# A new instruction order for all engines, with GpSimd's first load behind the identity and the integer positions

## The chip, the cores and the metric

The kernel runs on one core of a Trainium2 chip. The metric is the device time of one execution in microseconds, as the median of several runs. The engines are TensorE (PE, with its weight loads as PEld), VectorE (DVE), ScalarE (ACT), GpSimd (POOL) and SyncE (SP); each works through its own list of instructions in order and waits on semaphores for the others.

## The reference

Two stages in a row: attention over a sliding window of 128 keys with a linear bias by distance, and then a token mixer whose weights come from the attention's own output.

```python
# attention: batch 8, heads 8, 576 positions, head size 64
scores = q @ k.T / 8 + slope[h] * -(i - j)        # only where 0 <= i - j < 128
attn   = softmax(scores)
x      = (attn @ v), heads side by side           # batch 8, 576, 512
# mixer
wq, wk = x @ w_q, x @ w_k                         # 512 -> 64
mixed  = ((wq @ wk.T) / 8) @ x
out    = relu(mixed) @ w_out                      # 512 x 512, float32
```

The kernel takes float32 and computes in float16 with float32 sums.

## The kernel before, in words

The work is cut by batch (0 to 7) and, in a batch, by blocks of 128 positions. The names below are those of the operations in the code; `X b.n` means operation X of batch b, block n.

- **Loads.** GpSimd issues nearly all of them: `Lq`, `Lk`, `Lv` for queries, keys and values, `Lt` for the tails (positions 512 to 575) of two batches, `Lw`, `Lwo` for weights. They cast to float16 on the way. Eight of them may be in flight: each waits for the landing of the one eight places ahead. The first blocks of batch 0 (`LF`) come as float32 on the queues of ACT and SP.
- **Transposes.** PE transposes queries and keys (`TF` and `TJ` in batch 0, then `TQ`, `TK`, `TT`); ACT or DVE evicts each result to `qkT` (`EF`, `EJ`, `ETQ`, `ETK`, `ETT`).
- **Softmax.** `QK` makes the scores of one block and half the heads in two banks of PSUM; `EXP` on ACT turns them into exponentials (64 of them, line 657); `MUL` on DVE multiplies by the exponential of the bias, with zero outside the window (32, line 672). That factor, `bias`, is made once: GpSimd writes integer distances (`iota`), DVE turns them into `wm` (`wmc`), ACT takes eight exponentials. `PV` multiplies with the values and with a column of ones (`ones`), which gives the row sums; `RC` and `X` on DVE divide.
- **Mixer**, for two batches at a time: `XT`, `XTT` transpose x; `WQ`, `WK`, `WT` project; `G` is wk.T @ x; `MX` the mixed rows; `RM`, `RMT` the relu; `OUT` the last product; `EO` its eviction; `DO` the store. The last output block is stored as two halves, `OUT7.3a` and `OUT7.3b`.
- `WM` are matmuls on zeros that keep PE busy; `ident` is the identity as float32, `idh` its float16 copy; `zeros` and `pads` are fills.

PSUM is four pairs of banks; `P21` behind a PE operation in the order is pair 2, bank 1, and `P2` the whole pair.

The order of everything is one text, `ORDER`: a list of `name:engine`. `Order.follow` emits the operations in exactly this order, so each engine's list is the subsequence with its letter (P, A, D, G for GpSimd, S for SP). The dependencies of an operation, given as a list in the code, become semaphore waits. Which engine evicts what is part of the text too. The durations given beside the operations in the code do nothing when the kernel is built.

```python
def load(name, want, emits, n, deps):
    return add(*name, want, {"POOL": (0.95 * len(emits), 0.95 * len(emits) + 4.8)}, [ident, *deps],
               lambda o: [e() for e in emits])
```

This helper (line 289) makes every GpSimd load. Its list of dependencies names `ident`, the making of the identity on GpSimd itself.

Of the kernel before, what the change touches and what calls it, by code (L numbers as in the profile page):

```python
# [78 lines left out]
OUT1.1:P31 RC3.0:D RC3.1:D Lk4.2:G X3.1:D EO0.1:A QK4.1.0:P2 X3.0:D TQ5:P1 Lt2:G EXP4.1.0:A
XT3.0:P30 ETQ5:D PV3.2:P0 EO1.1:A PV3.3:P2 EXT3.0:A Lv4.1:G RC3.2:D OUT1.2:P31 X3.2:D Lv4.0:G  # L80
RC3.3:D X3.3:D QK4.0.0:P0 TK5.0:P1 Lk5.2:G EXP4.0.0:A PV3.4:P30 ETK5.0:D XT3.1:P20 Lk5.3:G
RC3.4:D EO1.2:A X3.4:D QK5.0.0:P0 QK5.1.0:P1 MUL4.1:D XTT2:P3 EXP5.0.0:A Lv5.1:G OUT0.0:P21
EXP5.1.0:A EXT3.1:D Lk6.3:G OUT0.3:P00 EXTT2:D EO0.0:A Lk6.2:G MUL4.0:D QK5.0.1:P1 TK4.1:P3
EO0.3:A TT4:P2 Lv5.0:G EXP5.0.1:A OUT1.0:P01 ETK4.1:D Lk6.0:G ETT5:D ETT4:A QK4.2.1:P3 MUL5.0:D
# [12 lines left out]
MUL6.2:D ETT7:A PV5.2:P1 EXP6.0.1:A Lv6.2:G OUT3.2:P30 RC5.2:D ETT6:D X5.2:D Lv7.3:G EO2.2:A
PV5.4:P20 EO3.2:A MUL6.0:D QK6.3.0:P0 TQ7:P1 Lv7.4:G EXP6.3.0:A QK6.1.1:P3 Lv7.0:G OUT3.1:P21
RC5.4:D ETQ7:D EXP6.1.1:A PV5.3:P0 EO3.1:A QK7.0.0:P1 RC5.3:D X5.4:D OUT2.0:P30 Lv6.3:G
EXP7.0.0:A X5.3:D MX2.4:P2 QK7.1.0:P0 EO2.0:A QK6.3.1:P1 RMT2:D EXP7.1.0:A XT5.1:P31 Lv7.2:G  # L100
DO2.0:S MUL6.1:D OUT3.0:P30 DO1.1:S EXP6.3.1:A Lv7.1:G DO1.0:S TK7.1:P0 EXT5.1:D DO1.4:S
QK7.0.1:P2 EO3.0:A PV6.1:P1 ETK7.1:D DO1.2:S EXP7.0.1:A XTT4:P3 DO0.3:S RC6.1:D PV6.2:P0 X6.1:D
DO3.3:S EXTT4:A QK7.3.1:P2 RC6.2:D DO0.0:S MUL7.0:D QK7.3.0:P1 EXP7.3.1:A WK4:P30 DO3.0:S
DO2.2:S EXP7.3.0:A X6.2:D PV6.0:P2 WT4:P31 RC6.0:D MUL6.3:D EWK4:A QK7.2.1:P0 QK7.1.1:P1 EWT4:A
WQ4:P30 X6.0:D EXP7.1.1:A G4:P31 MUL7.3:D EXP7.2.1:A PV6.4:P10 EWQ4:D EG4:A PV7.4:P11
QK7.2.0:P0 RC6.4:D RC7.4:D MX4.4:P3 X7.4:D PV6.3:P2 EXP7.2.0:A X6.4:D OUT3.4:P11 RC6.3:D RMT4:A
X6.3:D MX4.0:P0 MUL7.2:D EO3.4:A MX4.1:P3 XTT6:P2 RM4.0:A XT6.1:P10 DO3.4:S OUT5.4:P11 EXTT6:D
DO3.2:S RM4.1:A MUL7.1:D PV7.3:P0 EO5.4:A MX4.2:P2 RC7.3:D MX4.3:P3 X7.3:D RM4.2:A DO5.4:S
WT6:P11 EXT6.1:D PV7.2:P0 RM4.3:A EWT6:D PV7.1:P2 XT6.0:P10 RC7.2:D X7.2:D OUT4.1:P11 EXT6.0:A
RC7.1:D X7.1:D PV7.0:P0 OUT4.2:P30 RC7.0:D X7.0:D XT7.1:P10 XT7.0:P31 EXT7.1:D OUT5.2:P00  # L110
EXT7.0:A OUT5.3:P10 EO4.1:A WK6:P31 DO4.1:S EO5.3:D DO3.1:S WQ6:P01 EWK6:A EO4.2:A G6:P31
EWQ6:A DO4.2:S DO2.3:S OUT5.0:P01 EG6:A EO5.2:A MX6.0:P3 MX6.4:P1 DO5.2:S MX6.3:P2 RM6.0:D
RMT6:A OUT4.3:P00 EO5.0:A RM6.3:D MX6.1:P1 DO5.0:S EO4.3:A MX6.2:P3 OUT4.0:P01 RM6.2:A DO4.3:S
RM6.1:D DO5.3:S OUT5.1:P00 EO4.0:A OUT7.4:P30 DO4.0:S EO5.1:A OUT7.2:P01 DO5.1:S EO7.4:A
# [960 lines left out]
```

## Time and profile before

| | |
|---|---|
| median of 3 runs | 139.48 us (139.01, 139.48, 140.8) |
| the profiled execution | 138.34 us, of it 136.4 us from its first to its last instruction (the span) |
| TensorE clock granted | 0.993 of full |
| PE busy | 121.7 us (89%) |
| ACT busy | 115.2 us (85%) |
| DVE busy | 107.2 us (79%) |
| GpSimd busy (it issues loads) | 86.3 us (63%) |
| DMA | 24.97 MB, mean 183 GB/s |

The costliest groups are the 64 exponentials on ACT (62.7 us), the 32 multiplications by the bias factor on DVE (38.4 us) and the last product on PE (31.3 us). In the rows of the profile a number in brackets at the end is the time that the engine sat idle before the instruction and what ended it; "issue" means that nothing the profile shows was waited for. In the table of stages each row gives the stretch, its length, the busy time and count of PE, PEld, DVE, ACT and POOL, the granted clock, the share of the DMA engines and GB/s.

### The profile page before, as it was taken

The page shows a single profiled execution, that of the slowest core. Times are in us where ns is not written, and L with a number is a line of the kernel's source. Part 1 is how long each engine was busy: PE and PEld are TensorE (multiplying, and loading weights), DVE is VectorE, ACT ScalarE, POOL GpSimd, SP SyncE. Part 2 cuts the span into 40 slices and gives each one's busy share as a digit, 9 for nine tenths or more (in the row PEclk, how much of TensorE's full clock was granted, in tenths as well). Part 3 has the DMA queues.
Part 4 walks back from the last instruction along what each step waited for, and adds up shares of the span by engine and source line. Part 5 has one row for each costly group of instructions (what it writes and reads, how often), then busy time and mean ns, then how long its engine had stood idle before and what let it go on. Part 6 is the DMA issues. An engine that isn't in the chain of part 4 may idle for free.

```text
span 136.4 us, 5056 instructions
## 1 busy us (share of the span) xinstructions
PE 121.7 (89%) x2173; PEld 78.7 (58%) x2173; DVE 107.2 (79%) x187; ACT 115.2 (85%) x155; POOL 86.3 (63%) x108
## 2 busy tenths in 40 slices
PE   6696797898989799999999999999996999999980
PEld 1453465676757576576486685655765576634440
DVE  4338899999799999999999999997987996245200
ACT  2687998999999999998999998999998684678460
POOL 7999969499969948999999999995100000000000
PEclk9999999999999999999999999999999999999997
DMA  4999999999999999999999999999999570458894
GB/s 99 215 174 169 159 152 183 161 157 142 167 158 170 190 182 153 157 154 157 155 157 153 156 159 143 205 253 177 184 316 361 140 203 0 154 231 304 261 362 154
DMA packets 105414, 24.97 MB, mean 183 GB/s; under 512 B 95536, under 2 KB 100912, under 8 KB 105392
## 3 DMA queue, kind: packets, MB, share of 16 engines
q0 software_dynamic: 96832, 14.42, 149.7%
q1 hardware_dynamic: 6400, 9.05, 19.6%
q10 hardware_dynamic: 2160, 1.18, 2.9%
q8 instruction: 17, 0.28, 0.8%
q14 instruction: 5, 0.04, 0.1%
HBM read 29.62 MB, written 9.44 MB: 286 GB/s over the span
## 4 chain that ended last, share of the span: by engine, by line
PE 49%; DVE 25%; ACT 13%; issue 6%; DMA 3%; SPq 1%; ACTq 0%; DVEq 0%
PE pair L240 40%; DVE pt L672 9%; PE pair L243 9%; ACT pt L657 9%; DVE qkT L254 6%; DVE x L733 5%; DMA osb<-in_q_dram 3%; ACT qkT L252 3%; DVE rm L888 2%; DVE inv L723 1%; ACT osb L252 1%; DVE xT L254 1%; SPq L412 1%; DVE gs L254 1%; DVE xTt L254 0%
## 5 line engine op out<-in xcount | busy, mean ns | idle before, releaser
L657 ACT ACTIVATE pt<-pair 128x1024 f16<-128x1024 f32 x64 | 62.7, 1035 | 3.5 <-PE pair L240 2.6
L393 POOL DMA_DIRECT2D vt<-in_v_dram x40 | 35.7, 962 | 5.5 <-DMA natk<-in_k_dram 2.0
L672 DVE TENSOR_TENSOR pt<-pt,bias 128x2048 f16<-128x2048 f16 x32 | 38.4, 1212 | 0.0
L240 PE MATMUL pair<-wout_sb,rm 128*128 128x512 f16 (+1 forms) x132 | 31.3, 373 | 0.0
L367 POOL DMA_DIRECT2D natk<-in_k_dram x31 | 28.5, 956 | 1.3 <-DMA vt<-in_v_dram 1.1
L240 PE MATMUL pair<-qkT 64*128 64x256 f16 (+2 forms) x320 | 22.6, 250 | 3.7 <-DVE qkT L254 2.6
L240 PE MATMUL pair<-vt,pt 128*128 128x65 f16 (+1 forms) x576 | 22.3, 194 | 3.1 <-issue 0.9
L240 PEld LDWEIGHTS <-pt 128*128 128x128 f16 (+1 forms) x576 | 19.3, 100 | 9.0 <-issue 6.1
L733 DVE TENSOR_TENSOR x<-pair,inv 128x512 f16<-128x512 f32 x32 | 22.0, 689 | 0.9
L252 ACT COPY osb<-pair 128x512 f32<-128x512 f32 (+1 forms) x31 | 17.6, 581 | 4.8 <-PE pair L240 4.2
L240 PEld LDWEIGHTS <-rm 128*128 128x128 f16 x132 | 11.5, 98 | 11.9 <-issue 1.6
L254 DVE COPY qkT<-pair 128x1024 f16<-128x1024 f16 (+2 forms) x25 | 17.3, 700 | 1.3 <-PE pair L243 1.0
L240 PEld LDWEIGHTS <-qkT 64*128 64x128 f16 x320 | 11.4, 94 | 10.7 <-issue 5.0
L379 POOL DMA_DIRECT2D natq<-in_q_dram x12 | 11.5, 1024 | 1.9 <-DMA natq<-in_q_dram 1.6
L886 ACT ACTIVATE rm<-pair 128x1024 f16<-128x1024 f32 x11 | 10.8, 1025 | 0.1
L243 PE MATMUL pair<-identh,x 128*128 128x128 f16 x128 | 9.7, 219 | 0.4 <-DVE x L733 0.4
L252 ACT COPY qkT<-pair 128x1024 f16<-128x1024 f16 (+2 forms) x8 | 8.5, 1088 | 0.9 <-PE pair L243 0.6
L888 DVE TENSOR_SCALAR rm<-pair 128x1024 f16<-128x1024 f32 x5 | 5.9, 1220 | 3.9 <-PE pair L240 3.9
L243 PEld LDWEIGHTS <-x 128*128 128x128 f16 x128 | 7.7, 97 | 2.2 <-issue 1.0
L252 ACT COPY xT<-pair 128x1024 f16<-128x1024 f16 x6 | 6.2, 1027 | 2.9 <-PE pair L243 2.9
L723 DVE RECIPROCAL inv<-pair 128x8 f32<-128x8 f32 x32 | 6.3, 200 | 2.3 <-PE pair L240 1.7
L240 PE MATMUL pair<-warm 128*128 128x512 f16 x21 | 6.6, 439 | 1.3 <-DVE warm L295 1.2
(69 smaller groups left out, 136.9 us busy)
## 6 DMA issues: line engine op xcount, KB each, us to landing
out_dram<-osb SPq DMA_DIRECT2D x29, 256.0 KB, 4.0
vt<-in_v_dram POOLq DMA_DIRECT2D x32, 128.0 KB, 7.1
natk<-in_k_dram POOLq DMA_DIRECT2D x31, 128.0 KB, 6.5
natq<-in_q_dram POOLq DMA_DIRECT2D x4, 512.0 KB, 7.6
natq<-in_q_dram POOLq DMA_DIRECT2D x12, 128.0 KB, 5.7
out_dram<-osb SPq DMA_DIRECT2D x8, 128.0 KB, 2.5
vt<-in_v_dram POOLq DMA_DIRECT2D x8, 64.0 KB, 5.3
natt<-in_q_dram POOLq DMA_DIRECT2D x4, 128.0 KB, 5.7
```

The source lines that it names most:

```text
L240: hold(nc.tensor.matmul(*a, **k))
L243: hold(nc.tensor.transpose(*a))
L252: hold(nc.scalar.copy(out_ap, in_ap))
L254: hold(nc.vector.tensor_copy(out=out_ap, in_=in_ap))
L367: return lambda: nc.gpsimd.dma_start(out=natk(b, n), in_=k[b, :, P * n:P * n + P, :].transpose([1, 0, 2]))
L379: return lambda: nc.gpsimd.dma_start(out=rows_q(b)[:, r], in_=q[b, :, 0:512, :].rearrange("h (p r) d -> r p h d", r=QR)[r])
L393: return lambda: nc.gpsimd.dma_start(out=vtv(b, t)[:n, :, 0:D], in_=v[b, :, P * t:P * t + n, :].transpose([1, 0, 2]))
L657: nc.scalar.activation(out=pt, in_=two(hold_.bank).rearrange("p e c -> p (e c)"), func=AF.Exp, scale=SCALE)
L672: nc.vector.tensor_tensor(out=pv, in0=pv, in1=bt, op=ALU.mult)
L733: nc.vector.tensor_tensor(out=x_s[b % NX][qt].rearrange("p (g h d) -> p g h d", g=2, h=4), in0=sums(p)[:, :, :, 0:64], in1=box["inv"].unsq ...
L886: hold(nc.scalar.activation(out=out_ap, in_=in_ap, func=AF.Relu, scale=WSCALE))
L888: hold(nc.vector.tensor_scalar(out=out_ap, in0=in_ap, scalar1=0.0, scalar2=WSCALE, op0=ALU.max, op1=ALU.mult))
```

## The change

Three edits. Each load names `iota` as a dependency beside `ident`. The numbers of `WM` matmuls per place are others (22 in all instead of 21). And `ORDER` is a new text: the same 693 operations in another order, with 44 of them on another engine or queue. Of the evictions of the last product (`EO`), 24 instead of 31 are on ACT and 13 instead of 6 on DVE. The order was found by a search in whose model an instruction fetch takes long until the loads have ended; nothing of that search is in the kernel.

```diff
-WARM = (5, 10, 1, 2, 1, 2,)
+WARM = (6, 9, 1, 1, 2, 3,)
...
     def load(name, want, emits, n, deps):
-        return add(*name, want, {...}, [ident, *deps],
+        return add(*name, want, {...}, [ident, iota, *deps],
```

The start of the order:

```diff
-warm:D LF0.0.0.0:A LF0.0.1.0:S ones.2:D ident:G LF0.0.0.1:A LF0.1.0.1:S LF0.0.1.1:A ones.3:D
-LF0.1.0.0:S Lv2.4:G iota:G Lq0.2:G wmc:D Lk0.2:G WM.0:P31 TF0.0.0:P00 ones.0:D Lk0.1:G
-TF0.1.1:P01 EF0.0.0:A Lq1.0:G bias:A TF0.1.0:P00 Lk1.0:G EF0.1.0:D idh:D Lk1.1:G ones.1:D
-Lv0.1:G WM.1:P31 TJ0.2.0:P00 EF0.1.1:A Lv0.0:G TF0.0.1:P10 EJ0.2.0:A QK0.0.0:P2 Lk1.2:G
-EF0.0.1:D EXP0.0.0:A pads:D TJ0.1.1:P3 QK0.0.1:P1 Lk1.3:G TJ0.2.1:P0 zeros:D EXP0.0.1:A
+warm:D LF0.0.0.0:A LF0.0.1.0:S ones.2:D iota:G LF0.0.1.1:A LF0.1.0.0:S ident:G LF0.0.0.1:A
+zeros:D LF0.1.0.1:S Lv2.4:G ones.1:D Lq0.2:G pads:D Lk0.2:G wmc:D WM.0:P31 TF0.0.0:P00 Lk0.1:G
+ones.3:D bias:A Lq1.0:G ones.0:D TF0.0.1:P01 idh:D Lk1.0:G TF0.1.1:P10 EF0.0.1:D Lk1.1:G
+TF0.1.0:P11 EF0.1.1:D Lv0.0:G EF0.0.0:A EF0.1.0:A Lk1.2:G Lk1.3:G WM.1:P31 TJ0.2.1:P1
+QK0.0.1:P0 QK0.0.0:P2 EJ0.2.1:D Lv0.1:G TJ0.2.0:P30 EXP0.0.0:A TJ0.1.1:P1 EJ0.2.0:D Lk0.3:G
+EXP0.0.1:A QK0.2.1:P3 EJ0.1.1:D QK0.2.0:P2 QK0.1.1:P1 EXP0.2.1:A MUL0.0:D TQ1:P0 EXP0.2.0:A
```

PE alone, from the projection WK4 of batches 4 and 5 to the first products of batch 7:

```diff
-WK4 PV6.0 WT4 QK7.2.1 QK7.1.1 WQ4 G4 PV6.4 PV7.4 QK7.2.0 MX4.4 PV6.3 OUT3.4 MX4.0 MX4.1
-XTT6 XT6.1 OUT5.4 PV7.3 MX4.2 MX4.3 WT6 PV7.2 PV7.1 XT6.0 OUT4.1 PV7.0
+WK4 PV6.1 PV6.2 QK7.3.0 WQ4 PV6.4 QK7.3.1 QK7.2.1 QK7.2.0 G4 PV6.3 OUT3.4 PV7.4 MX4.4 MX4.1
+MX4.0 XT6.0 OUT5.4 MX4.2 XTT6 MX4.3 XT6.1 WT6 PV7.2 PV7.3 OUT4.2 PV7.0
```

The loads from the last of batch 6's keys on, with the stores that open the store queue:

```diff
-... Lq7.03 Lk7.3 DO2.1 Lk7.2 DO1.3 DO0.1 Lv6.0 DO0.2 Lv6.1 Lv6.2 Lv7.3 Lv7.4 Lv7.0 Lv6.3 Lv7.2 DO2.0 DO1.1 Lv7.1 DO1.0 ...
+... Lv7.3 Lk7.2 Lk7.3 Lv6.2 Lv6.0 DO3.3 Lv6.1 DO0.2 DO2.1 Lv6.3 DO0.1 DO1.3 Lv6.4 DO1.0 Lv7.0 DO0.0 Lv7.4 Lv7.2 Lv7.1 DO3.0 ...
```

The end of the order:

```diff
-EO7.0:A OUT7.3a:P30 EO7.3b:A DO7.0:S DO7.3b:A EO7.3a:A DO7.3a:A
+DO6.1:S EO6.3:D OUT7.1:P30 DO6.3:S EO7.0:A OUT7.3b:P10 DO7.0:S EO7.1:A OUT7.3a:P11 EO7.3b:D
+DO7.1:S DO7.3b:A EO7.3a:A DO7.3a:S
```

More of the change, by code (lines that the diff above doesn't have):

```diff
@@ L79 @@
[L79 to L84, printed above, removed]
@@ L97 @@
[L97 to L102, printed above, removed]
@@ L103 @@
[L103 to L114, printed above, removed]
@@ new lines @@
+TK4.1:P3 OUT0.3:P21 EXP5.0.0:A Lk6.0:G ETK4.1:D TT4:P1 EO0.0:D EO0.3:A Lq6.02:G XTT2:P3
+QK5.1.1:P0 ETT5:D ETT4:A OUT1.0:P20 EXTT2:D Lk6.2:G EXP5.1.1:A MUL4.1:D PV4.0:P3 Lk6.1:G
+QK4.2.0:P1 EO1.0:A QK4.2.1:P0 RC4.0:D WK2:P21 EXP4.2.0:A X4.0:D Lv5.1:G MUL5.1:D OUT1.4:P20
+EXP4.2.1:A Lk6.3:G PV4.1:P1 MUL5.0:D EWK2:A Lq6.01:G EO1.4:A TK5.1:P0 QK4.3.0:P3 Lv4.3:G
+WQ2:P21 RC4.1:D EXP4.3.0:A X4.1:D Lq6.00:G ETK5.1:D WT2:P20 EWQ2:A QK4.3.1:P3 MUL4.2:D EWT2:A
+Lq6.03:G QK5.2.0:P0 PV5.0:P1 EXP4.3.1:A G2:P20 Lk7.0:G RC5.0:D X5.0:D EXP5.2.0:A Lv4.4:G
@@ new lines @@
+MUL4.3:D QK5.2.1:P3 XT4.0:P21 EG2:A Lk7.1:G PV4.2:P0 EXP5.2.1:A EXT4.0:D MX2.3:P1 Lq7.02:G
+RC4.2:D MX2.2:P2 RM2.3:A X4.2:D TK6.1:P3 Lt3:G ETK6.1:D TK6.0:P0 RM2.2:A PV5.1:P1 ETK6.0:D
+MX2.0:P3 RC5.1:D PV4.3:P0 Lq7.01:G X5.1:D RM2.0:A QK5.3.1:P2 RC4.3:D TQ6:P1 Lv5.2:G X4.3:D
+EXP5.3.1:A MX2.1:P3 ETQ6:D QK5.3.0:P0 Lq7.03:G RM2.1:A XT4.1:P20 Lq7.00:G PV4.4:P21 EXT4.1:D
+EXP5.3.0:A TK7.0:P1 QK6.1.0:P3 Lv5.4:G ETK7.0:D OUT3.3:P20 EXP6.1.0:A RC4.4:D Lv5.3:G X4.4:D
+QK6.1.1:P1 MUL5.2:D QK6.2.1:P0 QK6.2.0:P3 Lv7.3:G EXP6.1.1:A OUT2.1:P21 Lk7.2:G EXP6.2.0:A
@@ new lines @@
+XT5.0:P10 OUT2.3:P11 Lk7.3:G EO2.1:A EXT5.0:D EXP6.2.1:A MUL5.3:D PV5.2:P3 Lv6.2:G OUT2.2:P10
+EO3.3:A Lv6.0:G RC5.2:D EO2.3:A DO3.3:S X5.2:D TT6:P2 EO2.2:A TQ7:P0 Lv6.1:G DO0.2:S ETT6:D
+QK6.0.1:P3 ETT7:D DO2.1:S QK6.0.0:P1 ETQ7:D Lv6.3:G EXP6.0.1:A PV5.4:P20 DO0.1:S OUT3.2:P21
+DO1.3:S Lv6.4:G EXP6.0.0:A RC5.4:D DO1.0:S MUL6.1:D QK6.3.0:P0 Lv7.0:G DO0.0:S PV5.3:P3
+EXP6.3.0:A OUT3.1:P10 X5.4:D Lv7.4:G RC5.3:D EO3.2:A X5.3:D Lv7.2:G QK6.3.1:P0 EO3.1:A
+QK7.1.0:P2 MUL6.0:D MX2.4:P3 EXP6.3.1:A XT5.1:P11 Lv7.1:G OUT2.0:P10 RMT2:D EXP7.1.0:A EXT5.1:D
@@ new lines @@
+TK7.1:P0 QK7.0.0:P3 EO2.0:A XTT4:P2 MUL6.2:D OUT3.0:P11 EXTT4:A EXP7.0.0:A ETK7.1:D WT4:P10
+QK7.1.1:P2 MUL6.3:D EWT4:A QK7.0.1:P3 PV6.0:P0 EXP7.1.1:A WK4:P10 RC6.0:D X6.0:D EXP7.0.1:A
+PV6.1:P2 MUL7.1:D PV6.2:P0 EO3.0:A QK7.3.0:P3 EWK4:A RC6.2:D DO3.0:S RC6.1:D WQ4:P11 X6.2:D
+EXP7.3.0:A DO1.1:S X6.1:D PV6.4:P10 DO1.2:S EWQ4:A QK7.3.1:P0 DO2.3:S RC6.4:D QK7.2.1:P2 X6.4:D
+QK7.2.0:P3 EXP7.3.1:A DO0.3:S MUL7.0:D G4:P11 DO1.4:S EXP7.2.1:A DO2.2:S MUL7.3:D PV6.3:P0
+DO2.0:S EG4:A OUT3.4:P10 DO3.1:S EXP7.2.0:A RC6.3:D X6.3:D PV7.4:P11 EO3.4:A MX4.4:P2 MX4.1:P3
@@ new lines @@
+RC7.4:D MX4.0:P0 X7.4:D RMT4:A XT6.0:P10 RM4.1:D RM4.0:A OUT5.4:P11 EXT6.0:D MX4.2:P0 EO5.4:A
+XTT6:P3 MX4.3:P2 MUL7.2:D EXTT6:A XT6.1:P10 RM4.3:A WT6:P11 RM4.2:D PV7.2:P3 EXT6.1:A PV7.3:P2
+EWT6:D OUT4.2:P00 RC7.2:D X7.2:D PV7.0:P1 OUT5.3:P01 RC7.3:D RC7.0:D X7.3:D PV7.1:P3 X7.0:D
+XT7.1:P20 RC7.1:D OUT4.3:P10 X7.1:D EO5.3:D XT7.0:P11 EO4.3:A OUT4.1:P21 DO5.3:S EXT7.0:D
+EXT7.1:A DO5.4:S EO4.2:D OUT5.1:P10 DO3.2:S WK6:P20 EO5.1:D DO5.1:S WQ6:P10 EWK6:A DO3.4:S
+G6:P20 EWQ6:D OUT5.0:P10 EG6:A EO4.1:A MX6.4:P0 MX6.0:P3 EO5.0:D DO4.1:S MX6.3:P2 RM6.0:A
@@ L289, in load @@
     def load(name, want, emits, n, deps):
-        return add(*name, want, {"POOL": (0.95 * len(emits), 0.95 * len(emits) + 4.8)}, [ident, *deps],
+        return add(*name, want, {"POOL": (0.95 * len(emits), 0.95 * len(emits) + 4.8)}, [ident, iota, *deps],
                    lambda o: [e() for e in emits])
```

68 lines of the change are left out of this document (30 added, 38 removed).

## The prediction

> **What bounds the kernel now.** I read the page first (busy time, queues), then a table of stages, then the start instruction by instruction, then the loads and the one long unexplained pause of PE.
>
> ```profile
> span 136.4 us, 5056 instructions
> ...
> PE 121.7 (89%) x2173; PEld 78.7 (58%) x2173; DVE 107.2 (79%) x187; ACT 115.2 (85%) x155; POOL 86.3 (63%) x108
> ...
> q8 instruction: 17, 0.28, 0.8%
> ```
>
> The stages below are cut where the work changes: start, first softmax stage, second, last, tail. Each pair after the length is an engine's busy time and its instruction count.
>
> ```profile
> 0.00:16.00 16.00, 11.68 (x147) 6.60 (x148) 8.85 (x25) 10.87 (x17) 14.93 (x24) 1.00 1.61 163
> 16.00:62.00 46.00, 41.40 (x886) 29.15 (x885) 43.86 (x71) 44.11 (x53) 39.02 (x48) 1.00 2.16 164
> 62.00:89.50 27.50, 26.95 (x526) 17.71 (x516) 26.75 (x45) 26.42 (x36) 27.50 (x33) 1.00 2.34 163
> 89.50:110.40 20.90, 19.73 (x421) 13.37 (x421) 18.51 (x33) 18.96 (x28) 4.81 (x6) 1.00 1.50 240
> 110.40:132.40 22.00, 21.96 (x204) 11.88 (x203) 9.23 (x16) 14.50 (x24) 0.00 (x0) 1.00 0.59 210
> ```
>
> The order is PE, weight load, DVE, ACT, POOL. No engine bounds everything. From 16 to 62 us DVE (43.86 of 46) and ACT (44.11) are both nearly full; from 62 to 89.5 us PE, DVE, ACT and POOL all are; in the tail PE alone is (21.96 of 22.00). What a new order can win is the idle time of the start, some two microseconds of DVE and ACT idle between 89.5 and 110.4 us, and nothing in the tail.
>
> The loads run close ahead of their users. One key block of batch 5 and the transposes (TK5.0) that use it:
>
> ```profile
> L367 POOL DMA_DIRECT2D natk<-in_k_dram x1: 896/896/896, 55.0 to 55.0; - x1
> ...
> DMA to landing us min/median/max: 6.3/6.3/6.3
> ...
> 61.73 0.40 PE L243 MATMUL pair<-identh,natk 64*128 64x64 f16 x16
> ```
>
> Issued at 55.0, landed at 61.3, used at 61.73: 0.4 us of slack. PE does not wait, but work that came earlier here would.
>
> **The start.** The change puts the two iotas ahead of the identity and the first load behind both, and reorders DVE, ACT and PE.
>
> ```profile
> 1.25 0.28 DVE L321 MEMSET vt<- 64x264 uint32 x1
> 1.44 0.81 POOL L393 DMA_DIRECT2D vt<-in_v_dram  x1
> ...
> 1.74 0.09 DVE L322 MEMSET vt<- 128x40 f16 x1 [0.21 <-DVE vt L321]
> ...
> 2.26 0.39 POOL L309 IOTA wint<- 128x256 int32 x1
> ...
> 2.58 0.27 POOL L310 IOTA wint<- 128x128 int32 x1
> 2.76 0.75 POOL L371 DMA_DIRECT2D natq<-in_q_dram  x1
> 2.88 0.36 DVE L316 TENSOR_SCALAR wm<-wint 128x384 f32<-128x384 int32 x1 [0.37 <-POOL wint L310]
> ...
> 3.86 0.56 DVE L318 SCALAR_TENSOR_TENSOR wm<-wm,wint 128x384 f32<-128x384 f32 x1
> ...
> 5.41 3.41 ACT L336 ACTIVATE bias<-wm 128x384 f16<-128x384 f32 x8
> ...
> 10.51 0.69 DVE L254 CAST qkT<-pair 128x512 f16<-128x512 f32 x1 [1.85 <-PE pair L243]
> ...
> 10.84 1.94 ACT L657 ACTIVATE pt<-pair 128x1024 f16<-128x1024 f32 x2
> ...
> 11.87 0.55 DVE L326 MEMSET qkT<- 128x256 uint32 x2
> ...
> 12.75 0.94 PE L240 MATMUL pair<-qkT 64*128 64x256 f16 x12 [0.99 <-DVE qkT L254]
> ...
> 13.51 1.02 ACT L657 ACTIVATE pt<-pair 128x1024 f16<-128x1024 f32 x1 [0.73 <-PE pair L240]
> ```
>
> GpSimd: both iotas together fill 2.26 to 2.85, so the first load moves from 1.44 to about 2.03. It was followed by the iotas before, and is followed by the query tail's load at once now: 2.03 + 0.81 = 2.84 against 2.76. Every later load therefore moves by 0.1 us at most. The one that is really late by 0.6 us is the last value block of batch 2, which nothing uses before batch 2's last product. Cost: 0 to 0.1.
>
> DVE: the positions are ready some 1.4 us earlier, but `wmc` now stands behind two `ones` (0.58 each, 1.25 to 1.83), `zeros` (0.55) and `pads` (four small memsets; 0.6 is an estimate from the one at 1.74 and the gap before it): 1.25 + 0.58 + 0.55 + 0.58 + 0.6 = 3.6, and its three steps (2.88 to 4.42, 1.54) end at 5.2 instead of 4.42. ACT no longer evicts a transpose ahead of the bias, so the eight exponentials run 5.2 to 8.6 instead of 5.41 to 8.82. Behind them come the two evictions (0.6 and 0.35, estimates from the casts in this stage) and one QK (0.39 per four matmuls): the first EXP starts near 10.05 instead of 10.84.
>
> The third EXP now waits for 32 small transposes (0.7) and one cast (0.69) behind that QK: 10.0 + 0.7 + 0.7 + 0.4 gives 11.9, which is before the second EXP ends at 12.0. The 0.73 us of ACT idle at 13.51 goes, and so does the 0.99 us that PE waited at 12.75, since `pads` and `zeros` no longer stand between it and the DVE copies. I carry the first EXP's 0.8 us as the head start; the bounds are 0 (the bias chain is late by what I estimated for `pads`) and 1.5 (the third EXP).
>
> **Where the head start goes.** Up to the last product of batch 3 the new order moves evictions between ACT and DVE: four of keys or queries or x (0.68, 0.70, 1.23, 0.69), two of 0.42 come to DVE, five (0.68, 0.69, three of 0.42) leave it, by the means of these shapes: 4.14 - 2.63 = +1.5 us for DVE, about -3 for ACT. DVE then has 43.86 + 1.5 = 45.4 us of work. At the share it reaches in the next stage (26.75 of 27.5, 97.3%) that needs 46.6 us, 0.6 more than the 46 of now. Head start -0.8, plus 0.6: -0.2 at 62 us. The loads say the same from the other side: the first 50 keep their places to within a few, batch 5's first keys stand at the same place, and their slack is 0.4, less 0.1 for the later start. I take **-0.25**, with ends of -0.4 (slack used up) and +0.8 (DVE only as full as now, 43.86 of 46, 95.3%: 47.6 us needed, +1.6, less 0.8). From 62 to 89.5 us the lists hold the same work on all engines to within 1 us: 0.
>
> **The pause of PE.** Between 89.5 and 110.4 us PE stops once for long, and names nothing that it waits for:
>
> ```profile
> 96.31 0.66 PE L240 MATMUL pair<-vt,pt 128*128 128x65 f16 x16
> ...
> 97.73 0.73 PE L240 MATMUL pair<-qkT 64*128 64x192 f16 x16
> ...
> 98.39 1.11 PE L240 MATMUL pair<-wqk_sb,xT 128*128 128x64 f16 x32
> ...
> 100.73 1.05 PE L240 MATMUL pair<-xT,wqk_sb 128*64 128x512 f16 x8
> ...
> 101.61 1.03 PE L240 MATMUL pair<-x,wk 128*64 128x512 f16 x8
> ...
> 102.48 0.39 PE L240 MATMUL pair<-xtl,wkt 128*64 128x256 f16 x4
> 102.70 0.42 PE L240 MATMUL pair<-vt,pt 128*64 128x65 f16 x16
> ...
> 103.69 0.39 PE L240 MATMUL pair<-qkT 64*128 64x256 f16 x4
> ...
> 105.33 0.57 PE L240 MATMUL pair<-vt,pt 128*128 128x65 f16 x13 [0.92 <-issue]
> ...
> 105.73 1.02 PE L240 MATMUL pair<-wout_sb,rmt 128*128 128x512 f16 x4
> ```
>
> It stops inside one product (three of its 16 matmuls before, 13 after), so no operand is missing. I read it as a late block of instructions: the instruction queue moved 17 blocks of 16 KB (0.28 MB), and PE has 2 x 2173 = 4346 instructions, 256 to a block, that is 128 matmuls with their weights. The block that ended here began some 12 matmuls into WK4 (98.39). It was used up at 104.41 = 105.33 - 0.92, 6.02 us after WK4's start; the next one was there after 6.94.
>
> In the new order the block starts in WK4 too, but holds other work: WK4 1.11, PV6.1, PV6.2 and PV6.3 0.66 each, two QK of group 3 0.73, WQ4 1.05, G4 1.03 + 0.39, PV6.4 0.42, two QK 0.39 each, OUT3.4 1.02, and ends at PV7.4. That sums to 8.5 us. The operations that fill it now (WK4, PV6.0, WT4, two QK, WQ4, G4, PV6.4, PV7.4, a QK, MX4.4) sum to 7.15 by their rows and took 6.02, since neighbours overlap; at the same ratio 8.5 becomes 7.15. That is more than 6.94: the fetch fits by 0.2 us, and the pause goes. DVE and ACT both idle around it, so it lies on the path. Gain **-0.9**; ends -0.9 and 0.
>
> The Trainium skill's page "Runtime: NRT & Kernel Launch" (Instruction fetch mechanics) says that the next block is fetched while the current one runs, 256 instructions at a time, and that crossing into it is mostly hidden; the block size agrees with this trace, "hidden" does not agree with the 0.92. By that rule the pause has another cause, the gain is 0, and the sum is -0.25.
>
> **The tail** after 110.4 us holds the same PE work in both orders from PV7.2 on, but that PV7.3 stands there in place of XT6.0 (0.66 against some 0.6); PE has no idle to give. Seven evictions move from ACT to DVE, which has 12.8 us free there (22.00 - 9.23): 0. Of the last two half stores ACT still issues one ahead of its last eviction: 0 to -0.1.
>
> **Sum.** -0.25 - 0.9 = -1.15: span 136.4 to 135.25. The profiled execution's own time is 138.34, of which 1.94 lies around the span, so 137.2. The median of the runs shown is 139.48, 1.14 above the profiled one; the same step from there gives **138.3 us**.
>
> **Rivals.**
>
> *More stores ahead of the last loads (slower).* The store queue opens with four stores now, behind which it waits; with seven in the new order.
>
> ```profile
> natq<-in_q_dram POOLq DMA_DIRECT2D x12, 128.0 KB, 5.7
> ...
> 85.33 2.55 SPq L993 DMA_DIRECT2D out_dram<-osb  x4
> ...
> L393 POOL DMA_DIRECT2D vt<-in_v_dram x1: 1191/1191/1191, 86.3 to 86.3; - x1
> ...
> DMA to landing us min/median/max: 8.4/8.4/8.4
> ```
>
> The value load issued at 86.3 behind four stores took 8.4 us instead of 5.7: 0.7 a store, 2.0 for three more. It landed at 94.7, the next some 0.9 later, and the product at 96.31 needs both: 0.7 of slack. So +1.3 once batch 6's value loads land later than their product's turn, and the fetch stays late behind the same traffic: -0.25 + 1.3 is +1.05, **140.5**. Against it: the store queue now opens behind a later eviction, by then about three more loads are through. 0.2.
>
> *DVE takes over* in 16 to 62 us: +0.8 - 0.9 = -0.1, **139.4**. For it: DVE would have 0.6 us idle in 46. 0.12.
>
> *The pause is no late fetch, or moves to another block's end*: only -0.25, **139.2**. For it: the margin of 0.2 us; and the page named above. 0.16.
>
> *The order runs as planned in the last two stages as well*: -0.4 at 62, and ACT's idle of 1.08 + 1.94 = 3.0 between 62 and 110.4 falls to 1.0, pause included, -2.0: **137.1**. For it: ACT and DVE still wait some 1 us there beside the pause. 0.17.
>
> **How the numbers follow.** The forecast has 0.35. The two nearest rivals lie between it and no change, so 137.1 to 140.5 are the cases; with 0.6 beyond either end for the spread of the runs (139.01 to 140.8 before) the range is 136.4 to 141.0. A measurement of this kernel tells about 2% from no change, here 2.8 us: under 136.7 is reached only if the fast rival goes somewhat further, 0.12; over 142.3 only if the stores cost twice what I gave them, 0.07; within 0.81.
>
> **What would show it.** Right: the first EXP near 10.0 us, no ACT idle of 0.7 before the third; DVE over 97% busy from 16 to 62 us; TK5.0 at 61.3 to 61.6; PE without a pause named "issue" over 0.3 us after 95 us; the tail from PV7.2 as long as now (22 us). Wrong: PE waiting for value loads near 97 us with landings over 9 us; a pause of 0.5 us or more at another place between 85 and 110; or a DVE stretch over 98% from which ACT idles longer than now.

## The result, and the profile after

The new kernel takes 137.91 us (median of 20 runs, 136.91 to 139.82) against 138.97 us for the kernel before in the same session (20 runs, 137.66 to 141.44): a ratio of 0.9929, interval 0.99 to 0.9958. That is 1.06 us less, inside the two per cent that count as no change. Ratios, here and below, compare only the executions in the faster of the two states in which each kernel runs, so they differ a little from the ratios of the medians. The forecast was 1.2 us less. The profiled execution took 137.62 us, 135.4 us of it the span.

The page of the new kernel, the lines that answer to those shown of before, and the share of the engines in the chain that ended last, below it the same line of before:

```profile
span 135.4 us, 5054 instructions
...
PE 122.8 (91%) x2174; PEld 78.1 (58%) x2174; DVE 114.0 (84%) x197; ACT 107.3 (79%) x145; POOL 86.3 (64%) x108
...
q8 instruction: 17, 0.28, 0.8%
...
PE 67%; DVE 13%; ACT 10%; DMA 3%; issue 3%; ACTq 1%; DVEq 0%
```

```profile
PE 49%; DVE 25%; ACT 13%; issue 6%; DMA 3%; SPq 1%; ACTq 0%; DVEq 0%
```

Some 7 us of work moved from ACT to DVE (ACT has 7.9 us less, DVE 6.8 more). In the chain PE has 67% (49% before), DVE 13% (25%) and "issue" 3% (6%). The same five stretches in the table of stages:

```profile
0.00:16.00 16.00, 12.30 (x142) 7.09 (x144) 8.65 (x26) 9.41 (x16) 14.73 (x24) 1.00 1.60 162
16.00:62.00 46.00, 41.60 (x904) 29.07 (x898) 44.81 (x72) 42.75 (x53) 39.48 (x48) 1.00 2.17 165
62.00:89.50 27.50, 27.06 (x549) 17.39 (x549) 25.53 (x43) 26.44 (x37) 27.50 (x33) 1.00 2.41 154
89.50:110.40 20.90, 20.87 (x414) 13.70 (x414) 20.57 (x33) 20.49 (x30) 4.63 (x6) 1.00 1.36 253
110.40:132.40 22.00, 20.92 (x180) 10.80 (x178) 14.40 (x26) 8.18 (x13) 0.00 (x0) 1.00 0.64 222
```

In 16 to 62 us DVE is at 44.81 of 46, which is 97.4%. In 89.5 to 110.4 PE is at 20.87 of 20.90 (19.73 before): there the pause is gone.

The start did not go as forecast. TensorE's timeline, and then ACT's, in the new kernel (start, duration, the group, and the idle time with what ended it):

```profile
3.80 1.10 PE L243 MATMUL pair<-ident,osb 128*128 128x128 f32 x4
6.56 2.02 PE L243 MATMUL pair<-ident,osb 128*128 128x128 f32 x8 [1.65 <-DMA osb<-in_q_dram]
8.40 2.92 PE L240 MATMUL pair<-warm 128*128 128x512 f16 x9
11.25 0.29 PE L243 MATMUL pair<-identh,natk 64*128 64x64 f16 x8
```

```profile
5.12 3.41 ACT L336 ACTIVATE bias<-wm 128x384 f16<-128x384 f32 x8 [1.40 <-DVE wm L318]
8.44 0.83 ACT L252 CAST qkT<-pair 128x512 f16<-128x512 f32 x2
12.02 6.59 ACT L657 ACTIVATE pt<-pair 128x1024 f16<-128x1024 f32 x7 [2.75 <-PE pair L240]
```

The bias chain was early (5.12, forecast 5.2), but TF0.0.1 waited 1.65 us for a first block that landed at 6.51, and behind it nine zero matmuls stood ahead of the first QK. The first EXP came at 12.02, not 10.05, which is 1.18 us later than in before's profile (10.84). From it on, ACT runs without the 0.73 us gap ahead of the third EXP.

The block of instructions that starts in WK4, on TensorE's timeline, and the waits of PE from 60 us on, of the new kernel:

```profile
97.88 1.09 PE L240 MATMUL pair<-wqk_sb,xT 128*128 128x64 f16 x32
...
104.01 1.02 PE L240 MATMUL pair<-wout_sb,rmt 128*128 128x512 f16 x4
104.97 0.44 PE L240 MATMUL pair<-vt,pt 128*64 128x65 f16 x16
```

```profile
PE pair L240 <- ACT pt L657: 0.3, 1, 0.3
```

No "issue" is among them (0.9 before). Between the two profiled executions the difference comes late: TK5.0 starts at 61.60 (61.73 before), PV5.4 at 89.51 (89.53), PV7.2 at 109.15 (110.41), the last product OUT7.3a at 130.72 (131.77). The experiments show that this pair of executions isn't the whole story.

### The profile page after: what moved, and what is told of

Its sections match the earlier page's. It is cut to its first block, busy times and chain, and to the rows that moved or that the text cites. A ratio compares the mean times of both kernels' runs of the same rounds, so it can differ in the third digit from the quotient of the medians.

```text
span 135.4 us, 5054 instructions
## 1 busy us (share of the span) xinstructions
PE 122.8 (91%) x2174; PEld 78.1 (58%) x2174; DVE 114.0 (84%) x197; ACT 107.3 (79%) x145; POOL 86.3 (64%) x108
## 4 chain that ended last, share of the span: by engine, by line
PE 67%; DVE 13%; ACT 10%; DMA 3%; issue 3%; ACTq 1%; DVEq 0%
PE pair L240 54%; PE pair L243 12%; ACT pt L657 6%; DVE pt L672 4%; DVE qkT L254 4%; DMA osb<-in_q_dram 3%; DVE x L733 3%; ACT qkT L252 2%; DVE rm L888 1%; ACTq L412 1%; ACT rm L886 1%; DVE inv L723 1%; ACT wqT L252 0%; DVE xT L254 0%; ACT gs L252 0%
## 5 line engine op out<-in xcount | busy, mean ns | idle before, releaser
L254 DVE COPY qkT<-pair 128x1024 f16<-128x1024 f16 (+2 forms) x27 | 19.3, 734 | 4.1 <-PE pair L243 3.9
L252 ACT COPY osb<-pair 128x512 f32<-128x512 f32 (+1 forms) x24 | 14.0, 596 | 10.5 <-PE pair L240 9.7
L254 DVE COPY osb<-pair 128x512 f32<-128x512 f32 (+1 forms) x13 | 8.7, 668 | 5.1 <-PE pair L240 5.1
L240 PE MATMUL pair<-warm 128*128 128x512 f16 x22 | 7.8, 491 | 1.5 <-DVE warm L295 1.2
L254 DVE COPY xT<-pair 128x1024 f16<-128x1024 f16 x11 | 7.5, 685 | 1.2 <-PE pair L243 1.1
L243 PE MATMUL pair<-identh,natk 64*128 64x64 f16 x248 | 6.5, 191 | 1.2 <-ACT pt L657 0.9
L243 PEld LDWEIGHTS <-natk 64*128 64x128 f16 x248 | 5.3, 94 | 3.9 <-issue 3.3
```

The costliest lines, as they stand in the source:

```text
L240: hold(nc.tensor.matmul(*a, **k))
L243: hold(nc.tensor.transpose(*a))
L252: hold(nc.scalar.copy(out_ap, in_ap))
L254: hold(nc.vector.tensor_copy(out=out_ap, in_=in_ap))
```

## The experiments

Ratios are to the kernel before on the same chip, whose medians there were 139.02 us (e1 to e4), 139.02 us (e5, e6, h1, h2) and 138.77 us (e7, e8, h3, h4); the new kernel itself was not run beside them. Each kernel ran 12 times, e3, h2 and h4 six times. Where only places in the order change, the diff gives the moved words. Line numbers in the experiments are one lower than in the two kernels.

### The pause alone

**e1.** OUT3.4 is moved forward in the order of before, to lengthen the block:

```diff
-... G4 ... MX4.4 ... PV6.3 ... OUT3.4 ... EO3.4 ...
+... G4 OUT3.4 ... EG4 EO3.4 ... MX4.4 ... PV6.3 ...
```

> The order of before with one product moved: OUT3.4 (four matmuls, 1.02 us) and its eviction stand right behind G4 instead of behind PV6.3, so they lie inside the block of 256 PE instructions that starts in WK4 and ended in a pause of 0.92 us. Late fetch (my theory): the block takes about 0.9 us longer, the pause shrinks from 0.92 to under 0.2 us, and the kernel gains 0.6 to 0.9 us, ratio to before 0.993 to 0.996. Rival, the pause has another cause or PE was only waiting for others there: the pause stays or the idle time turns up elsewhere, ratio 0.998 to 1.002.

Measured: 139.68 us, ratio 1.0029 (0.9996 to 1.0063). The pause is gone from the profile, but two waits for ACT of 0.30 and 0.41 us stand in the same stage. The runs show no gain from the edit. That it took the pause away is not shown either: e5 and e6 below leave this stretch of before's order as it is, and their profiles have no pause. (The profiled execution of e1 ran at half the granted clock from 16.1 to 19.6 us, so I read its waits and not its sums.)

**e2.** Nine stores of before are moved behind DO3.4 on the store queue, so that the last loads have the DMA engines to themselves:

```diff
-... DO0.2 DO2.0 DO1.1 DO1.0 DO1.4 DO1.2 DO0.3 DO3.3 DO0.0 DO3.0 DO2.2 DO3.4 ...
+... DO0.2 DO1.1 DO3.4 DO2.0 DO1.0 DO1.4 DO1.2 DO0.3 DO3.3 DO0.0 DO3.0 DO2.2 ...
```

> The order of before with nine of the ten stores that run between 94 and 103 us moved behind DO3.4 on the store queue (about 107 us). Nothing else differs. Late fetch behind DMA traffic: with the stores gone from the queues the instruction block comes earlier than 6.9 us after the start of WK4, the pause is under 0.3 us, the last value loads land 2 to 4 us earlier than 109 us, and the gain is 0.5 to 0.9 us (ratio 0.993 to 0.996). Rival, the fetch takes as long without the stores (it is late by its own, and only a longer block cures it): the pause stays at 0.7 us or more and the ratio is 0.998 or above.

Measured: 139.53 us, ratio 1.0037 (1.0007 to 1.0068). The last load landed at 101.1 us instead of 109.1, and the pause moved one block ahead, into WK4 itself (TensorE's timeline of e2):

```profile
99.95 0.49 PE L239 MATMUL pair<-wqk_sb,xT 128*128 128x64 f16 x11
100.94 0.77 PE L239 MATMUL pair<-wqk_sb,xT 128*128 128x64 f16 x21 [0.50 <-issue]
```

Less traffic from stores doesn't cure it. One matmul group of equal operations is cut in two here, exactly 128 matmuls before the place of the pause in before: that fits the end of a block of instructions, as the prediction read it.

**e4.** The same step the other way: OUT3.4 is moved back in the new order.

```diff
-... PV6.3 ... OUT3.4 ... PV7.4 EO3.4 MX4.4 ...
+... PV6.3 ... PV7.4 MX4.4 OUT3.4 EO3.4 ...
```

> The changed kernel with OUT3.4 and its eviction moved out of the block of instructions again, from before PV7.4 to behind MX4.4. The block that starts in WK4 then takes about 6.1 us instead of 7.1. If the new order cured the pause by the length of the block: a pause named issue of 0.5 to 0.9 us comes back near PV7.4, and the ratio to before rises from 0.993 to 0.997 to 1.000. If it was cured because the stores stand elsewhere and the fetch itself comes earlier (it landed 4.3 us after the start of WK4 in the changed kernel, 5.5 in the one before): no pause over 0.2 us, ratio 0.991 to 0.995.

Measured: 138.89 us, ratio 0.9971 (0.9935 to 1.0006). TensorE's timeline of e4:

```profile
104.07 0.66 PE L239 MATMUL pair<-vt,pt 128*128 128x65 f16 x16
105.24 0.44 PE L239 MATMUL pair<-vt,pt 128*64 128x65 f16 x16 [0.51 <-DVE pt L671]
```

No pause comes back although the block is shorter again. Instead PV7.4 waits 0.51 us for MUL7.3. In the new order OUT3.4 covers that wait. From WK4 to PV7.2 this profile takes 12.31 us against 11.27 in the new kernel's, so the place of OUT3.4 is likely worth something, but not because it lengthens a block. The runs alone do not show it: the interval of e4 overlaps that of the new kernel.

### The start

**e3.** The new kernel with eight of the nine zero matmuls of the second place moved to the first.

```diff
-WARM = (6, 9, 1, 1, 2, 3,)
+WARM = (14, 1, 1, 1, 2, 3,)
```

> The changed kernel with eight of the nine matmuls on zeros that stand before the first key transposes (8.4 to 11.3 us) moved to the very start (14 there, 1 here; 22 in all, so the instruction blocks keep their places). The first EXP should start about 9.7 to 10.2 us instead of 12.0. Loads set the pace (my theory): by TK5.0 (61.60 us) the head start is down to 0.5 us or less, and the time is that of the changed kernel within 0.4 us, ratio to before 0.989 to 0.994. Rival, the head start is kept: 1.5 to 2 us less, ratio 0.978 to 0.983. A third way: PE runs colder in the first transposes and is slower, ratio above 0.995.

Measured: 136.91 us, ratio 0.9856 (0.9814 to 0.9899). That interval lies just below the new kernel's own (0.99 to 0.9958): with six runs, in another session than the new kernel's, this version beats before and very likely the new kernel too. TensorE's timeline of e3, then ACT's:

```profile
1.19 5.70 PE L239 MATMUL pair<-warm 128*128 128x512 f16 x14 [1.19 <-DVE warm L294]
6.73 2.44 PE L242 MATMUL pair<-ident,osb 128*128 128x128 f32 x12
8.99 0.40 PE L239 MATMUL pair<-warm 128*128 128x512 f16 x1
...
12.95 1.08 PE L242 MATMUL pair<-identh,natq 128*64 128x128 f16 x32 [0.34 <-DMA natq<-in_q_dram]
...
18.11 0.62 PE L242 MATMUL pair<-identh,natk 64*128 64x64 f16 x16 [1.11 <-DMA natk<-in_k_dram]
```

```profile
10.40 3.77 ACT L656 ACTIVATE pt<-pair 128x1024 f16<-128x1024 f32 x4 [0.82 <-PE pair L239]
```

The zeros fill the wait for the first blocks, the first EXP comes at 10.40, and then PE waits for loads (0.34 and 1.11 us), which the new kernel with its late start doesn't. TK5.0 comes at 61.86, no earlier than in the new kernel. But this profile shows e3 at its worst: the granted clock fell to half from 20.0 to 23.4 us, and of the six runs the profiled one is the slowest (138.13 us, the others 136.42 to 137.01). How far the others kept their lead no profile shows.

**e8.** The new kernel with eight of the same zeros left out.

```diff
-WARM = (6, 9, 1, 1, 2, 3,)
+WARM = (6, 1, 1, 1, 2, 3,)
```

> After with one zero matmul instead of nine at the second place (6, 1 instead of 6, 9; the variant with 14, 1 had the ratio 0.9856). Theory 1, the zeros only delay: the first EXP comes at 10.0 to 10.6 us, ratio 0.984 to 0.988, as good as with the zeros moved ahead. Theory 2, the zeros are needed to bring TensorE to its full rate early: the first EXP comes at 11 us or later, matmuls of the head take twice as long until some 13 us, ratio 0.993 to 1.000.

Measured: 138.18 us, ratio 0.9978 (0.9934 to 1.0021). TensorE's timeline of e8:

```profile
8.24 0.61 PE L239 MATMUL pair<-warm 128*128 128x512 f16 x1
9.32 0.40 PE L242 MATMUL pair<-identh,natk 64*128 64x64 f16 x8 [0.47 <-ACT qkT L251]
...
13.08 1.08 PE L242 MATMUL pair<-identh,natq 128*64 128x128 f16 x32 [0.42 <-DMA natq<-in_q_dram]
...
32.90 0.29 PE L242 MATMUL pair<-identh,natk 64*128 64x64 f16 x8 [0.33 <-DMA natk<-in_k_dram]
```

In its profile the start is as early as e3's (first EXP at 10.45) and loads are waited for as late as 32.90; its runs, on another chip, are not as good as e3's. Leaving the zeros out is not the same as running them earlier.

**e7.** The same for before.

```diff
-WARM = (5, 10, 1, 2, 1, 2,)
+WARM = (5, 1, 1, 2, 1, 2,)
```

> Before with one zero matmul instead of ten at the second place (WM.1), so that nothing stands in front of TJ0.2.0. Theory 1, these zeros delay work that is ready: TJ0.2.0 starts at about 8.0 us (its identity is made by 7.97) instead of 8.97 to 12.0, the first EXP comes near 10 to 10.8 us whichever rate TensorE has, and the ratio is 0.988 to 0.995. Theory 2, the zeros are what brings TensorE to its full rate; without them the transposes and QK of the head run at half rate to 13 us or more, and the ratio is 1.000 to 1.005.

Measured: 138.97 us, ratio 1.0048 (1.0009 to 1.0088). TensorE's timeline of e7:

```profile
8.06 1.06 PE L242 MATMUL pair<-identh,natq 64*64 64x64 f16 x32 [0.30 <-DVE identh L312]
...
10.12 0.61 PE L239 MATMUL pair<-qkT 64*128 64x256 f16 x4
...
13.86 1.92 PE L242 MATMUL pair<-identh,natq 128*64 128x128 f16 x32
```

The work starts earlier and runs at half speed: the same 32 transposes take 1.92 us here and 1.08 in e8's row, four QK 0.61 instead of 0.39. Here too the zeros cannot simply be left out; the first theory falls.

**e6.** Before with nine zeros moved to the first place.

```diff
-WARM = (5, 10, 1, 2, 1, 2,)
+WARM = (14, 1, 1, 2, 1, 2,)
```

> Before, with nine of the ten zero matmuls of the second place moved to the first (14, 1 instead of 5, 10). Theory 1, a start that is late passes through to the end, and what makes it late is the second group of zero matmuls in front of work that is ready (2.3 us in the profile of before, more where PE runs at the slow start-up rate): the first EXP comes no later than 10.8 us and the ratio is 0.993, the same step as between the new kernel with and without this edit (0.9856 against 0.9929). Theory 2, the step there came only from the new order's first transposes, which wait for a late landing in front of the zeros: ratio 1.000 here. Theory 3, in before the zeros are run in idle time of PE and the first group, grown by nine, delays TF0.0.0: 1.003 to 1.007.

Measured: 138.36 us, ratio 0.9974 (0.9938 to 1.001). ACT's timeline of e6:

```profile
7.63 0.59 ACT L251 CAST qkT<-pair 128x512 f16<-128x512 f32 x1 [3.92 <-PE pair L242]
8.11 3.42 ACT L335 ACTIVATE bias<-wm 128x384 f16<-128x384 f32 x8
```

In this order ACT evicts TF0.0.0 ahead of the bias, so the longer first group of zeros delays the bias from 5.41 to 8.11, and the first EXP comes at 12.59. In the new order the bias stands first and isn't touched. That would explain why the same edit gains 0.7% there and nothing certain here.

**e5.** Before with the iotas ahead of the identity, the part of the change in its title.

```diff
-... ident:G LF0.0.0.1:A ... LF0.1.0.0:S Lv2.4:G iota:G Lq0.2:G ...
+... iota:G ident:G LF0.0.0.1:A ... LF0.1.0.0:S Lv2.4:G Lq0.2:G ...
```

> Before, with only the two iotas put ahead of the identity on GpSimd; the first load then stands behind both, as in the new kernel. Theory 1, the head's lead is lost in front of the loads' pace: the eight bias exponentials start up to 0.7 us earlier (4.7 instead of 5.41), the first EXP at 10.1 to 10.8, TK5.0 at 61.5 to 61.8 as before, ratio 1.000. Theory 2, an early start passes to the end: ratio 0.995. Theory 3, the identity comes 0.6 us later and with it the first transposes and all loads: ratio 1.003 to 1.005.

Measured: 138.46 us, ratio 0.9975 (0.994 to 1.0009). By itself it gives nothing that can be told from no change: in this order the bias still stands behind EF0.0.0 and started at 5.45 (5.41 before). Its profile is of more use for what it shows of an execution of before's order. TensorE's timeline of e5, then ACT's; below them the one row of before's timeline that answers to it:

```profile
5.87 0.67 PE L242 MATMUL pair<-ident,osb 128*128 128x128 f32 x2 [0.50 <-DMA osb<-in_q_dram]
6.36 4.44 PE L239 MATMUL pair<-warm 128*128 128x512 f16 x10
10.72 0.69 PE L242 MATMUL pair<-identh,natq 64*64 64x64 f16 x32
...
99.97 1.11 PE L239 MATMUL pair<-wqk_sb,xT 128*128 128x64 f16 x32
...
106.22 1.02 PE L239 MATMUL pair<-wout_sb,rmt 128*128 128x512 f16 x4
```

```profile
12.59 1.94 ACT L656 ACTIVATE pt<-pair 128x1024 f16<-128x1024 f32 x2
15.27 3.77 ACT L656 ACTIVATE pt<-pair 128x1024 f16<-128x1024 f32 x4 [0.74 <-PE pair L239]
```

```profile
6.70 2.34 PE L240 MATMUL pair<-warm 128*128 128x512 f16 x10
```

The ten zeros take 4.44 us here and 2.34 in before's profile. PE's rate, and not the place of the iotas, makes the first EXP 1.75 us later: e2, whose start is that of before unchanged, has it at 12.57 with zeros that take 4.01 us. And in the last stage, in the same order of PE, there is no pause.

### Halves of the two orders

Four kernels take one order up to a cut and the other behind it. At the cuts, PV5.4 (some 89.5 us) and ETK1.0 (some 16 us), the two orders have done the same operations but for a few.

```diff
 h1: after's order up to PV5.4,  then before's
 h2: before's order up to PV5.4, then after's
 h3: after's order up to ETK1.0, then before's
 h4: before's order up to ETK1.0, then after's
```

> The order of after up to PV5.4, and from there that of before. Theory 1, the gain is made behind 89.5 us: ratio 1.000, PV5.4 to PV7.2 takes 20.9 us again. Theory 2, the gain is made earlier: ratio 0.993. Theory 3, each half fits only its own other half: 1.000 to 1.005.

> The order of before up to PV5.4 (about 89.5 us), and from there the order of after; both have done nearly the same operations by then. Theory 1, the whole gain is made behind 89.5 us by the new order of the last batches: the stretch from PV5.4 to PV7.2 shrinks from 20.9 to about 19.6 us, and the ratio is that of after, 0.993 (138.0 us). Theory 2, the gain is made earlier (head, loads, the move of evictions between ACT and DVE) and the profile that showed it late was one execution: ratio 1.000. Theory 3, the last stage's order only fits the state in which the new first part leaves the engines: a new wait at the seam, ratio 1.000 to 1.005.

> The order of after up to ETK1.0 (about 16 us), and from there that of before; the two have done nearly the same operations by then. Theory 1, the gain is made in the head: in most executions of before's order TensorE runs the ten zero matmuls at its slow start-up rate (0.43 us each) and the first EXP comes at 12.6 to 13.0 us, the third at 15.3 to 15.6; after's head has the third at 12.2 to 13.9, and the rest of before's order passes that on: TK5.0 before 62.5 us, ratio 0.990 to 0.995. Theory 2, the gain is made in the middle (evictions moved from ACT to DVE) or in the last stage: ratio 1.000. Theory 3, a new wait where the two orders meet: 1.000 to 1.005 with a gap near 16 to 20 us that names it.

> The order of before up to ETK1.0 (about 16 us), and from there that of after. Theory 1, the gain is made in the head: ratio 1.000, third EXP at 15.3 us or later in most executions, TK5.0 at 63 us. Theory 2, the gain is made in the middle or in the last stage: ratio 0.993, TK5.0 at 61.6 to 62 us in spite of the late head. Theory 3, a new wait where the two orders meet: 1.003 or more.

Measured: h1 140.13 us, ratio 1.0037 (0.9997 to 1.0078); h2 141.64 us, 1.0102 (1.0013 to 1.0191); h3 139.18 us, 1.0065 (1.0025 to 1.0105); h4 140.3 us, 1.0128 (1.0058 to 1.0198). (In h2 the mix changes what some operations behind the cut compute; which, I did not trace, and its time says little of the two orders.) None gains. h2, h3 and h4 lose, h1's interval just includes no change, and each profile shows waits that neither of the two kernels has there. TensorE's timelines of h1, h3 and h4:

```profile
100.50 0.76 PE L239 MATMUL pair<-wqk_sb,xT 128*128 128x64 f16 x20 [0.58 <-issue]
...
107.06 0.55 PE L239 MATMUL pair<-vt,pt 128*128 128x65 f16 x13 [1.27 <-issue]
```

```profile
17.38 0.38 PE L239 MATMUL pair<-warm 128*128 128x512 f16 x1 [0.90 <-DVE qkT L253]
```

```profile
19.54 0.38 PE L239 MATMUL pair<-warm 128*128 128x512 f16 x1 [1.42 <-ACT pt L656]
```

h2 has 1.31 and 0.59 us of waits for DVE at 94 to 97 us. So the third theory holds in kind in all four (in h2 and h3 the ratio lies above what it named), and they do not tell by themselves in which half the gain is made. h1 shows once more what a late fetch costs: 0.58 and 1.27 us at two block ends.

## Where the microsecond comes from

The profiles together tell more than the pair. This table gives start times from the timelines; "zeros" is the time of the ten (in the new start nine) zero matmuls of the second place where they stand there, "pause" the "issue" waits of PE behind 95 us, and the last column is the span less TK5.0. h1 and h2 change orders behind TK5.0, so that column is empty for them. e1 is left out: its clock fell to half at 16.1 us, and its TK5.0 came at 66.08.

| | zeros | first EXP | third EXP | TK5.0 | pause | TK5.0 to end |
|---|---|---|---|---|---|---|
| before | 2.34 | 10.84 | 13.51 | 61.73 | 0.92 | 74.7 |
| e2 (order of before) | 4.01 | 12.57 | 15.25 | 63.28 | 0.50 | 74.2 |
| e5 (order of before) | 4.44 | 12.59 | 15.27 | 63.30 | 0 | 73.8 |
| e6 (order of before) | - | 12.59 | 14.41 | 62.71 | 0 | 73.6 |
| e7 (order of before) | - | 10.77 | 13.55 | 62.65 | 0.57 | 74.2 |
| h3 (rest of before) | 3.44 | 12.25 | 14.07 | 62.68 | 0.52 | 74.2 |
| after | 2.92 | 12.02 | 13.85 | 61.60 | 0 | 73.8 |
| e3 (order of after) | - | 10.40 | 12.22 | 61.86 | 0 | 74.0 |
| e8 (order of after) | - | 10.45 | 12.27 | 61.18 | 0 | 74.6 |
| h4 (rest of after) | 4.11 | 13.04 | 15.72 | 64.29 | 0 | 73.7 |
| e4 (order of after up to OUT3.4) | 2.12 | 10.85 | 12.67 | 62.20 | 0 | 74.6 |
| h1 (order of after up to PV5.4) | 2.12 | 10.58 | 12.40 | 61.10 | 1.85 | |
| h2 (order of before up to PV5.4) | 4.36 | 12.96 | 15.63 | 63.68 | 0 | |

**Behind TK5.0 the two orders are equal within their spread**: 74.1 us on the mean of the first six rows, which run the order of before there (73.6 to 74.7), and 74.0 on the mean of after, e3, e8 and h4, which run that of after (73.7 to 74.6). e4, whose edit adds a wait of 0.51 us there, is in neither mean. A pause is in four of the six and in none of the four; what it costs, 0.42 us on the mean of the six, the new order gives back: from WK4 to PV7.2 it takes 11.27 us, before 12.02 with its pause, but e5 10.92 without one; and its tail from PV7.2 to the end takes 26.25 us instead of 25.99.

**Ahead of TK5.0 the new order is earlier in most executions.** Of the profiles that run one order with its own zeros up to there, those of before (before, e2, e5 but for the iotas, h2) have TK5.0 at 61.73, 63.28, 63.30 and 63.68, those of after (after, e4, h1) at 61.60, 62.20 and 61.10: 63.0 and 61.6 us on the mean, in seven executions. Whether the zeros of the second place run at 0.43 or at 0.21 us each changes from execution to execution. Where PE's first operations are those of before, they were slow in five of six profiles (e1, e2, e5, h2, h4: 4.01 to 4.45 us); before's own profile is the exception. With a slow start the first EXP comes at 12.57 to 13.04, the third at 15.25 to 15.72 (e2, e5, h2, h4; e1 later still), and in before's order TK5.0 at 63.3 to 63.7. The new kernel's own profile has a start that is slow in part (nine zeros in 2.92 us), and is there at 61.60: 0.6 us or more from the first EXP, 0.85 from the third's smaller distance (1.83 instead of 2.68), 0.3 from the third to TK5.0 (47.75 instead of 48.03). With a fast start loads are waited for, as in e3, e4 and e8, and little is left of the lead: e4 has TK5.0 0.47 us later than before's own profile.

One rival to this is open. The clock records of the trace begin at the moment at which PE's operations become fast: with before's first operations at 4.7 us in before and at 10.2 to 12.7 in e1, e2, e5, h2 and h4; with after's at 4.0, 5.1 and 5.3 us in h3, h1 and e4, and at 10.1 in after and e8. So part of the lead may come from the sixth zero of the first place, or be chance; that number was not changed alone. (In h3 the clock fell to half again from 7.4 to 10.8 us, which is why its zeros are slow.) The reading is drawn from the profiles; the kernels that were to prove it by swapping the halves were spoiled by their seams, so it stays the likeliest account and not a shown one. What the runs support best is that the start moves the time: e3 changes only the place of zeros, and its ratio is 0.7% below the new kernel's.

## Why the prediction was right or wrong

- **The number** (138.3 us; 137.91 came) and the range held. The two terms that made it did not come from where the prediction put them, so that the sum came so near is in good part luck.
- **The head start of 0.8 us** failed as worked out. The bias chain ended 8.53, as forecast (8.6). The step that failed is "Behind them come the two evictions [...] and one QK": the sum left out that TF0.0.1 waits for a landing at 6.51 and that nine zeros stand behind it, and it took PE's rate as given. In the two profiles the first EXP is 1.18 us later and not 0.8 earlier. (The terms as written also add up to 9.94, not 10.05, and those of the third EXP to 11.8, not 11.9.) The third EXP's gap of 0.73 went, as said.
- **The iotas and loads**: Lv2.4 moved from 1.44 to 1.85 us at its issue, Lq0.2 from 2.76 to 2.66. Cost 0, right.
- **The loads eat a head start**: right in the profiles with an early start of the new order. PE waits for loads, 0.34 and 1.11 us in e3, and TK5.0 stays at 61.1 to 62.2 in e3, e4, e8 and h1, with the first EXP at 10.4 to 10.9. In e3 the fall of the clock may have a part in that, and its runs gain in spite of it. The new kernel's own profile has 61.60, the top of the forecast 61.3 to 61.6, but no head start at the first EXP to lose.
- **DVE in 16 to 62 us** was to be over 97% busy: 44.81 of 46, 97.4%. Its work was 44.8 us, not 45.4, and it did not take over; that rival did not happen.
- **62 to 89.5 us**: from TK5.0 to PV5.4 27.91 us (27.80 before). Right.
- **The pause of 0.92 us as a late fetch**: right in kind, as far as the traces show. At all six such waits of 0.5 us or more in these profiles, PE goes on 1.4 to 1.6 us after the transfer of a block on the instruction queue has ended (before: the transfer starts at 102.9, takes 0.95, PE resumes at 105.33). The failed step is what decides it. "That is more than 6.94: the fetch fits by 0.2 us, and the pause goes" took the time of fetching as fixed; the block did take 7.09 us (WK4 to PV7.4), but e5 runs the old block in about 5.8 us from WK4 on, as before did (6.0), without a pause: the transfer began 2.2 us after WK4 and not 4.5. While loads run, a transfer starts anywhere between about 0 and 5 us after its block in these profiles; behind the last load it is near 0. So the pause varies with the execution, 0.42 us on the mean and not 0.92, and it can't be the gain that was put down to it. Why a transfer starts when it does stays open.
- The sentence of the Trainium skill weighed there ("Runtime: NRT & Kernel Launch", Instruction fetch mechanics: crossing a block is mostly hidden) holds for most block ends of a run (the queue moves 17 blocks) and not for all.
- **The tail**, forecast as unchanged from PV7.2, became 0.26 us longer in the two profiles.
- **Stores ahead of the last loads**, the slower rival: the mechanism is there, the price isn't. The last value loads took about 10 us to land (Lv7.1 issued at 92.90, landed at 103.07), but PE waited for none of them. *The order runs as planned* and *no late fetch* were wrong as stated; 137.1 and 139.2 lie on either side of what came.

## What to carry to other kernels

One profile of the kernel before is one execution: a wait in it that no dependency explains, or a start that hangs on TensorE's rate, may be absent from the next. Before costing the cure of such a wait, look at how much it can vary. Fill matmuls that keep TensorE busy did best in this kernel where it waits for data, in one unbroken run (e3), and ahead of nothing that another engine needs early (e6); the same zeros ahead of ready work delay it by the time they take, and leaving them out kept TensorE at half its rate for longer (e7).

## What the runs showed of the hardware

- TensorE starts at half its rate and changes at a moment that differs between executions. The zero matmuls of 128x512 take 0.43 us and then 0.21. With fourteen without a break from 1.19 us (e3) the change comes at about 6.3 us; in e5, with waits of 0.32 and 0.50 us in between, at about 10.7; in e7, with fewer zeros, only at about 17.8. The granted clock in the tables of stages reads 1.00 in all these stretches, so there this has to be read from durations; the trace's list of clock records, which those tables draw on, begins only with the change, at 6.30 us in e3, 10.65 in e5 and 17.82 in e7. The Trainium skill's page "TensorE: Matmul & The Clock Gate" (Part 1: The HAM clock gate) says that the rate doubles after some 4 us of sustained work, judged in windows of 3.4 us that run freely, so that the moment varies; the two rates agree (it gives 427 and 216 ns), the 5.1 us of e3 is somewhat longer than its figure.
- A half rate that comes later stands in e3's table of stages at a finer grain (the column behind POOL is the granted clock):

```profile
20.00:22.00 2.00, 2.00 (x36) 1.84 (x37) 1.97 (x4) 1.18 (x2) 2.00 (x3) 0.50 1.99 131
22.00:24.00 2.00, 1.73 (x37) 1.37 (x33) 1.97 (x4) 1.56 (x3) 2.00 (x4) 0.66 1.29 154
```

Here the granted clock fell to half for about 3.4 us (all of 20.00 to 22.00, and two thirds of the next two microseconds, whose mean is 0.66), soon after the wait of 1.11 us for a load at 18.11. The same fall, also for about 3.4 us, is in h3 from 7.4 and in e1 from 16.1 us. Why is not known; h4 waits 1.42 us at 19.54, and its granted clock reads 1.00 from 16 to 62 us.
